# Attention and MoE on one core: the DMA transpose of a step issued behind the next step's write

## The chip, the cores and the metric

The kernel runs on one core of a Trainium2 chip. The metric is device time in microseconds (us) of one execution, lower is better. The core has five engines with a queue each, worked through in order: PE (TensorE, matrix products), ACT (ScalarE), DVE (VectorE), POOL (GpSimd) and SP (SyncE, which here only issues DMAs). An engine that waits for a semaphore holds everything that is queued behind the waiting instruction.

## The reference

Two layers, 8 batches, 8 heads, 512 local and 32 global positions, 64 elements per head. First windowed attention:

```python
s_g = scale * q_g @ k_all.T              # 32 global rows see all 544 columns
out_g = softmax(s_g) @ v_all
s_ll = where(|i - j| <= 32, scale * q_l @ k_l.T, -1e9)
s_l = concat([scale * q_l @ k_g.T, s_ll])  # 512 local rows: 32 global columns and the band
out_l = softmax(s_l) @ concat([v_g, v_l])
```

Then, over the 4608 rows of both (512 wide, heads side by side), `h = x @ w_in` (512x2048), `g = h * sigmoid(h)`, `g @ w_out` (2048x512), all in float32 results.

## The kernel before, in words

**Tiles and steps.** The 4608 rows are 36 tiles of 128 rows, worked in 12 blocks (`SIZES`: ten of 3 tiles, two of 2). A local tile is one batch `b` and one quarter `c` of the 512 positions; it takes 4 steps, one for each pair of heads (`pr`). So there are 128 steps `k`, and 16 of them make a batch.

**One step.** Its queries and keys are loaded (L343 or L345, `raw`), and from step 28 on split into a rounded part and a remainder: ACT casts `qk` (L365), DVE makes `klo` (L366) and the remainder of the queries (L367). PE makes the scores `s` (L381, or L383 and L384), DVE adds the mask (L388), ACT takes the exponential (L392), ACT and DVE scale (L399, L401, L403). The result `probs` has to be transposed for the second product.

**The transpose through DRAM.** Up to step 11 PE does it. From step 12 on (`KF`), POOL copies `probs` into two 16-bit planes (`halves`, L413, one buffer), SP writes these to DRAM (`away`, L418), and SP issues a DMA transpose that reads them back turned, into `pt` (`st_back`, L422; four `pt` buffers, one for each `pr`). A transpose waits for its own write to have landed. The one of `pr` 0 also waits until PE has read the `pt` of the tile before. When all four `pt` of a tile are there, PE makes the tile's 32 products `o` (L464), and ACT and DVE put them into the block's `x` (L471, L472, L478).

**The global rows.** For each batch the 32 global rows' probabilities `pg` are made during the batch before, in two halves `hh` (L250 to L297). From batch 3 on (`GD`) they too go through DRAM: `gaway` (L310) and a DMA transpose into `pgt` (L329). A rest of 32 columns is turned by PE (`gu`, L332) and copied by ACT into `pgu` (L335, two copies for each half).

**The MoE.** For each of 16 slices `f` of a block PE makes `h` (L625, 12 matmuls), ACT takes the tanh `t` (L632), DVE makes the product (L633), ACT rounds it to `gh` (L635), DVE takes the remainder `gl` (L636), and PE adds the three products to `out` (L652, 9 matmuls) one slice later. `x` and the weights are used as a rounded part and a remainder as well. During block 0 the weights are still being joined from loaded words and split (L221 to L234).

**What sets the order.** Attention steps of later blocks are laid between the MoE matmuls. Each part of step `k` has a due time, `at` of the step plus a number from the tables `DUE`, `DMAT`, `DMAT0` (and `TURN`, `TURND` for the two halves of a batch's global transpose); all parts are sorted by it, and this list is the program's order. On PE, and for the issues of DMAs on SP (`hold`), that order stands. On ACT, DVE and POOL a scheduler that plays the program through with estimated times puts it into an order of its own. The change edits the tables alone, and the orders of ACT, DVE and POOL follow from them.

Of the kernel before, what the change touches and what calls it, by code (L numbers as in the profile page):

```python
# [23 lines left out]
NPR = H // 2  # L24
# [37 lines left out]

DUE = dict(load=-1.2, split=-0.5, turn=1.6, out=2.2)
DMAT = dict(load=-1.65, halves=0.7, away=1.05, turn=1.3, back=1.65, out=2.7)
DMAT0 = dict(turn=1.75, back=1.95)
VLOADS = (None, -0.6, -1.0, 2.4)
BEFORE = 1.36
HEAD = dict(load=-0.9, split=0.2, scores=0.8, soft=1.0, halves=1.4, away=1.72, slot=0.3, later=1.6)
HEADS0, HEADS = (11, 1), (7, 2)
TURN1, TURN, TURND = (0.65, 1.5), (0.4, 1.5), (0.4, 0.45)  # L70
FULL = 0.98
END = 0.5

# [1 line left out]
def attention_moe_kernel(ctx: ExitStack, tc: tile.TileContext, qk0_in, qk_in, v_in, gqk, wts, out):  # L75
# [443 lines left out]
    def put(when, fn, *a):  # L519
        stream.append((when, fn, a))  # L520
# [3 lines left out]
    for k, (t, b, c, pr) in enumerate(steps):  # L524
        a = (k, b, c, pr)
        j = k % NST
        due = dict(DUE)
        if k >= KF:
            due.update(DMAT)
            due.update({} if pr else DMAT0)  # L530
        if WHOLE <= k < WHOLE + OWN:
            due["load"] = SOONER
        if k < AHEAD:
            due.update({part: FIRST[part][k] - k for part in ("load", "vload", "turn", "out")})
        elif pr == 0:
            due["vload"] = VLOADS[min(k // NPR, 3)]
        if k == AHEAD:
            for h in range(NPR):
                put(FIRST["gload"][h], g_load, 0, h)
                put(FIRST["gscores"][h], g_scores, 0, h)  # L540
            for hh in range(2):
                put(FIRST["gsoft"][hh], g_soft, 0, hh)
                put(FIRST["gturn"][hh], g_turn, 0, hh)
            put(FIRST["late"], g_late)
            at = FIRST["then"]
            for when in JOINS:
                put(at + when - NPR, join_weights)
            for f, when in enumerate(SPLITS):
                put(at + when - NPR, split_weights, f)
        if j == 0 and b:  # L550
            for hh in range(2):
                put(at + (TURN1 if b < 2 else TURN if b < GD else TURND)[hh], g_turn, b, hh)
        for f, half in FIRSTW.get(k, ()):
            put(at + 0.01, fetch_weights, f, half)
        ats.append(at)
        put(min(at + due["load"], ats[k - 3] + BEFORE) if k >= ND + 3 else at + due["load"], st_load, *a)
        put(at + due["split"], st_split, *a)
        put(at, st_scores, *a)
        if "vload" in due:
            put(at + due["vload"], st_vload, *a)  # L560
        if k >= KF:
            put(at + due["halves"], st_halves, *a)
            put(at + due["away"], st_away, *a)
        put(at + due["turn"], st_turn, *a)
        if k >= KF:
            put(at + due["back"], st_back, *a)
        if k < SINGLE or pr == NPR - 1:
            n = 1 if k < SINGLE else NPR
            put(at + due["out"], st_out, k - n + 1, n, b, c, t)
            marks[t] = at + due["out"]  # L570
        if j == NST - 1 and b % 4 == 3:
            put(marks[t] + 0.001, g_tile, t + 1)
            marks[t + 1] = marks[t] + 0.001
        if b + 1 < B:
            first, every = HEADS if b > 1 else HEADS0
            for h in [h for h in range(NPR) if first + h * every == j]:
                for part, fn in (("load", g_load), ("split", g_split), ("scores", g_scores)):
                    put(at + (SOONER if part == "load" and b + 1 < GF else HEAD[part]), fn, b + 1, h)
                if h % 2:
                    put(at + HEAD["later" if b == 0 else "soft"], g_soft, b + 1, h // 2)  # L580
                    if b + 1 >= GD:
                        put(at + HEAD["halves"], g_halves, b + 1, h // 2)
                        put(at + HEAD["away"], g_away, b + 1, h // 2)
                at += HEAD["slot"]
        at += 1.0
# [180 lines left out]
```

## Time and profile before

| what | value |
|---|---|
| median of 3 runs | 965.2 us (964.59 to 966.34) |
| the profiled execution | 964.87 us, span of its instructions 962.7 us |
| PE busy | 940.6 us, 98% of the span |
| PEld (weight loads, beside PE) | 840.9 us, 87% |
| DVE, ACT, POOL busy | 629.9, 574.2, 217.1 us |
| granted PE clock | full in all slices but the last |
| HBM traffic | 133 GB/s over the span |

Steps 0 to 11 and the start of the weights take the first 50 us, block 0 runs to about 140 us and the rest to the end is a steady mixture of MoE and attention. In rows of the timeline the columns are start (us from the span's start), duration, engine, line, operation, what it writes from what it reads, how many, and in brackets how long the engine had been idle and who ended that. In rows of waits they are the engine and line, what it waited for, microseconds in total, how often, and the longest. SPq is SP's queue.

### The profile page before, as it was taken

How to read it: one execution, taken by the hardware profiler on the slowest of the kernel's cores; microseconds unless marked ns; L12 is line 12 of the kernel's file. 1: busy time of each engine (PE TensorE's matmuls, PEld its weight loads, DVE VectorE, ACT ScalarE, POOL GpSimd, SP SyncE). 2: the span in 40 equal slices, each digit the busy share in tenths (PEclk: the TensorE clock that was granted, in tenths of full speed). 3: DMA queues.
4: the chain of work that ended last, by engine and by line, in shares of the span. 5: the costliest groups of instructions: out<-in, count | busy, mean ns of one | idle time of the engine just before them, and what ended most of it. 6: DMA issues, size and time to landing. Idle time of an engine off the chain costs nothing.

```text
span 962.7 us, 17396 instructions
## 1 busy us (share of the span) xinstructions
PE 940.6 (98%) x5734; PEld 840.9 (87%) x5734; DVE 629.9 (65%) x1893; ACT 574.2 (60%) x1475; POOL 217.1 (23%) x433
## 2 busy tenths in 40 slices
PE   8789999999999999999999999999999999999998
PEld 6578888999998999989999899998999899989897
DVE  5889977766876677655677677766677656453322
ACT  7888876656656566544665656665566555443322
POOL 2112322122332223122133222222223221120000
PEclk9999999999999999999999999999999999999999
DMA  8989966577668675743856776686775864532000
GB/s 301 350 226 262 266 170 187 158 171 213 172 157 211 168 192 147 193 116 86 223 158 167 201 172 188 159 206 170 170 216 148 201 147 130 144 93 66 1 22 23
DMA packets 201306, 162.57 MB, mean 169 GB/s; under 512 B 139392, under 2 KB 159360, under 8 KB 201216
## 3 DMA queue, kind: packets, MB, share of 16 engines
q1 hardware_dynamic: 196800, 153.52, 59.9%
q10 hardware_dynamic: 4416, 7.93, 2.3%
q8 instruction: 46, 0.75, 0.3%
q14 instruction: 44, 0.36, 0.1%
HBM read 86.44 MB, written 41.94 MB: 133 GB/s over the span
## 4 chain that ended last, share of the span: by engine, by line
PE 83%; DVE 4%; ACT 2%; issue 1%; DMA 0%; DVEq 0%; ACTq 0%
PE h L625 36%; PE out L652 35%; PE o L464 6%; PE s L383 2%; PE s L384 2%; DVE w_lo L234 1%; DVE w L224 1%; PE gs L275 1%; PE gs L276 1%; DVE probs L388 1%; DVE klo L366 0%; DMA raw<-in_qk_dram 0%; DVE raw_w L223 0%; ACT probs L392 0%; DVE t L633 0%
## 5 line engine op out<-in xcount | busy, mean ns | idle before, releaser
L413 POOL COPY halves<-probs 128x512 uint16<-128x512 uint16 x232 | 154.9, 694 | 436.2 <-ACT probs L399 234.6
L632 ACT ACTIVATE t<-h 128x384 f32<-128x384 f32 (+1 forms) x192 | 90.6, 472 | 172.5 <-PE h L625 156.9
L633 DVE SCALAR_TENSOR_TENSOR t<-t,h 128x384 f32<-128x384 f32 (+1 forms) x192 | 101.6, 529 | 105.9 <-ACT t L632 104.8
L652 PE MATMUL out<-w_hi,gh 128*128 128x512 f32 x544 | 164.2, 400 | 2.5 <-ACT gh L635 2.5
L625 PE MATMUL h<-xh,w_hi 128*128 128x384 f32 (+1 forms) x768 | 160.0, 330 | 1.9 <-ACT w_hi L233 1.9
L652 PE MATMUL out<-w_lo,gh 128*128 128x512 f32 x544 | 161.2, 394 | 0.0
L652 PE MATMUL out<-w_hi,gl 128*128 128x512 f32 x544 | 161.0, 394 | 0.0
L625 PE MATMUL h<-xl,w_hi 128*128 128x384 f32 (+1 forms) x768 | 158.2, 327 | 0.0
L625 PE MATMUL h<-xh,w_lo 128*128 128x384 f32 (+1 forms) x768 | 158.2, 327 | 0.0
L392 ACT ACTIVATE probs<-probs,st 128x224 f32<-128x224 f32 x244 | 115.8, 475 | 62.8 <-DVE st L388 62.1
L625 PEld LDWEIGHTS h<-xh,w_hi 128*128 128x128 f32 x768 | 132.9, 188 | 17.4 <-ACT w_hi L233 3.6
L636 DVE TENSOR_TENSOR gl<-t,gh 128x384 fp32r<-128x384 f32 (+1 forms) x192 | 110.3, 575 | 43.1 <-ACT gh L635 40.9
L388 DVE CUSTOM_DVE_ANT_0 probs<-s,mask 128x224 f32<-128x224 f32 x244 | 85.8, 387 | 80.2 <-PE s L384 70.8
L625 PEld LDWEIGHTS h<-xl,w_hi 128*128 128x128 f32 x768 | 132.8, 188 | 0.0
L625 PEld LDWEIGHTS h<-xh,w_lo 128*128 128x128 f32 x768 | 131.3, 188 | 0.5 <-DVE w_lo L234 0.3
L635 ACT CAST gh<-t 128x384 fp32r<-128x384 f32 (+1 forms) x192 | 94.5, 492 | 57.8 <-DVE t L633 57.6
L652 PEld LDWEIGHTS out<-w_hi,gl 128*128 128x128 f32 x544 | 100.3, 188 | 22.2 <-DVE gl L636 0.5
L652 PEld LDWEIGHTS out<-w_lo,gh 128*128 128x128 f32 x544 | 100.5, 188 | 21.7 <-issue 0.6
L652 PEld LDWEIGHTS out<-w_hi,gh 128*128 128x128 f32 x544 | 93.8, 189 | 13.3 <-ACT gh L635 4.7
L365 ACT CAST qk<-raw 128x704 fp32r<-128x704 f32 x100 | 77.5, 775 | 7.7 <-DMA raw<-in_qk_dram 5.2
L366 DVE TENSOR_TENSOR klo<-raw,qk 128x448 fp32r<-128x448 f32 x100 | 66.2, 662 | 18.2 <-ACT qk L365 16.7
L399 ACT ACTIVATE probs<-probs,st 128x224 f32<-128x224 f32 x118 | 56.7, 481 | 30.2 <-DVE st L395 28.7
(96 smaller groups left out, 1065.7 us busy)
## 6 DMA issues: line engine op xcount, KB each, us to landing
raw<-in_qk_dram SPq DMA_DIRECT2D x100, 352.0 KB, 3.2
away<-halves SPq DMA_DIRECT2D x116, 256.0 KB, 2.3
vraw<-in_v_dram SPq DMA_DIRECT2D x30, 512.0 KB, 5.1
raw_w<-in_wts_dram SPq DMA_DIRECT2D x29, 512.0 KB, 6.4
raw_g<-in_gqk_dram SPq DMA_DIRECT2D x32, 304.0 KB, 3.1
out_dram<-o ACTq DMA_DIRECT2D x29, 256.0 KB, 3.3
raw<-in_qk_dram SPq DMA_DIRECT2D x28, 240.0 KB, 4.6
gaway<-pg SPq DMA_DIRECT2D x10, 256.0 KB, 2.1
```

Of the source, the lines that this page charges most:

```text
L365: nc.scalar.copy(out=qk, in_=raw)
L366: nc.vector.tensor_tensor(out=klo[:, :KW], in0=raw[:, QW:], in1=qk[:, QW:].bitcast(F32), op=ALU.subtract)
L388: nc.vector.tensor_tensor_reduce(out=p[:, u, :W], in0=ss[u], in1=mask_of[c], scale=-SCALE, scalar=3.0e38, op0=ALU.add, op1=ALU.min, accum_ ...
L392: nc.scalar.activation(p[:, u, :W], p[:, u, :W], AF.Exp, bias=st[:, u : u + 1], scale=-1.0, accum_out=st[:, 2 + u : 3 + u])
L413: nc.gpsimd.tensor_copy(out=halves[:, :, u], in_=p[:, 2 * P * u : 2 * P * (u + 1)].bitcast(U16).rearrange("p (j h) -> p h j", h=2))
L464: nc.tensor.matmul(o[D * u : D * (u + 1), :m], vraw[:, a, u, :], pt[:, u, a, :m], start=(a == 0), stop=(a == 1))
L625: nc.tensor.matmul(h[:, :nt], wt[:, c * P : (c + 1) * P], x[:, c, :nt], start=(i == 0), stop=(i == 3 * NCC - 1))
L632: nc.scalar.activation(t[:, :nt], h[:, :nt], AF.Tanh, scale=0.5)
L633: nc.vector.scalar_tensor_tensor(out=t[:, :nt], in0=t[:, :nt], scalar=1.0, in1=h[:, :nt], op0=ALU.add, op1=ALU.mult)
L635: nc.scalar.copy(out=gh[:, :nt], in_=t[:, :nt])
L636: nc.vector.tensor_tensor(out=gl[:, :nt], in0=t[:, :nt], in1=gh[:, :nt].bitcast(F32), op=ALU.subtract)
L652: nc.tensor.matmul(outs[n][i], g[:, i * P : (i + 1) * P], w, start=(f == 0 and j == 0), stop=(f == NF - 1 and j == 2))
```

## The change

Three numbers of the tables. `back`, the issue of a step's DMA transpose, was due 1.65 steps after the step's own place (1.95 for `pr` 0), and is now due at 2.1, except for `pr` 3, the last of a tile, where it stays at 1.65. The next step's write `away` is due at 1 + 1.05 = 2.05. So the transposes of `pr` 0, 1 and 2 stand behind the next step's write. And the second half of the global transpose is due at 1.5 instead of 0.45, a step later than the first, from batch 3 on. It takes with it the DMA transpose into `pgt`, PE's `gu` and ACT's two `pgu` copies.

```diff
 DMAT = dict(load=-1.65, halves=0.7, away=1.05, turn=1.3, back=1.65, out=2.7)
-DMAT0 = dict(turn=1.75, back=1.95)
+DMAT0 = dict(turn=1.75)
+BACK = 2.1
...
-TURN1, TURN, TURND = (0.65, 1.5), (0.4, 1.5), (0.4, 0.45)
+TURN1, TURN, TURND = (0.65, 1.5), (0.4, 1.5), (0.4, 1.5)
...
         if k >= KF:
             due.update(DMAT)
             due.update({} if pr else DMAT0)
+            if pr < NPR - 1:
+                due["back"] = BACK
```

No instruction is added or taken away on PE; five `gu` transposes stand elsewhere. In the rows of the changed kernel the line numbers are 1 higher up to `st_back` and the like and 3 higher from the step loop on (L366 is L365 of before, L635 is L632, L423 is L422). The numbers behind an underscore at a name's end are the program's own, and the number in a name is the step, as in `raw29`, `qk50`, or block and slice, as in `t8_9`.

First place: SP's queue at steps 24 to 30, around 137 to 157 us. Before:

```order
L418 DMA away25_1786<-halves25_1766 128x1024
L241 DMA raw_g2_0_1788<-in_gqk_dram 128x608
L355 DMA vraw24_1817<-in_v_dram 128x4x256
L670 DMA out_dram<-o0_1846 128x512
L422 DMA_TRANSPOSE pt1_130<-away25_1786 128x4x256
L345 DMA raw28_1823<-in_qk_dram 128x704
L670 DMA out_dram<-o0_1846 128x512 x2
L418 DMA away26_1873<-halves26_1825 128x1024
L241 DMA raw_g2_1_1881<-in_gqk_dram 128x608
L422 DMA_TRANSPOSE pt2_131<-away26_1873 128x4x256
L345 DMA raw29_1934<-in_qk_dram 128x704
L418 DMA away27_1936<-halves27_1893 128x1024
```

And now:

```order
L423 DMA_TRANSPOSE pt0_129<-away24_1709 128x4x256
L242 DMA raw_g2_0_1788<-in_gqk_dram 128x608
L356 DMA vraw24_1817<-in_v_dram 128x4x256
L346 DMA raw28_1822<-in_qk_dram 128x704
L673 DMA out_dram<-o0_1845 128x512 x3
L419 DMA away26_1872<-halves26_1824 128x1024
L423 DMA_TRANSPOSE pt1_130<-away25_1785 128x4x256
L242 DMA raw_g2_1_1881<-in_gqk_dram 128x608
L346 DMA raw29_1933<-in_qk_dram 128x704
L419 DMA away27_1935<-halves27_1892 128x1024
L423 DMA_TRANSPOSE pt2_131<-away26_1872 128x4x256
L423 DMA_TRANSPOSE pt3_132<-away27_1935 128x4x256
```

The load `raw28` no longer stands behind a transpose and an output, and the load `raw29` no longer behind the transpose that waits for `away26` to land.

Second place: ACT's queue at steps 48 to 50, around 289 to 301 us, where batch 3's first tile begins (the second row and the third come once more where the first "..." stands). Before:

```order
L632 ACTIVATE t2_13_3598<-h2_13_3585 128x384
L392 ACTIVATE probs0_85,st48_3610<-probs0_85,st48_3610 128x224
L335 COPY pgu3_3629<-gu3_0_3631 32x64
...
L335 COPY pgu3_3629<-gu3_1_3636 32x64 x2
L635 CAST gh2_13_3599<-t2_13_3598 128x384
L399 ACTIVATE probs0_85<-probs0_85,st48_3610 128x224
L365 CAST qk49_3640<-raw49_3565 128x704
...
L399 ACTIVATE probs1_86<-probs1_86,st49_3680 128x224
L365 CAST qk50_3702<-raw50_3623 128x704
L632 ACTIVATE t2_15_3720<-h2_15_3707 128x384
```

And now:

```order
L635 ACTIVATE t2_13_3597<-h2_13_3584 128x384
L393 ACTIVATE probs0_85,st48_3609<-probs0_85,st48_3609 128x224
L336 COPY pgu3_3629<-gu3_0_3631 32x64
...
L638 CAST gh2_13_3598<-t2_13_3597 128x384
L400 ACTIVATE probs0_85<-probs0_85,st48_3609 128x224
L366 CAST qk49_3635<-raw49_3565 128x704
...
L400 ACTIVATE probs1_86<-probs1_86,st49_3675 128x224
L336 COPY pgu3_3629<-gu3_1_3698 32x64 x2
L635 ACTIVATE t2_15_3720<-h2_15_3707 128x384
L366 CAST qk50_3702<-raw50_3623 128x704
L638 CAST gh2_15_3721<-t2_15_3720 128x384
```

Two of the four `pgu` copies have moved a step on, and there the cast `qk50` now stands behind the tanh `t2_15`. At steps 80 to 82 (batch 5) the rows have moved in the same way.

Third place: ACT's queue at steps 112 and 113, around 749 to 753 us, the first tile of batch 7. Before:

```order
L635 CAST gh8_8_8947<-t8_8_8946 128x384
L335 COPY pgu7_8980<-gu7_0_8982 32x64 x2
L399 ACTIVATE probs0_85<-probs0_85,st112_8958 128x224
L335 COPY pgu7_8980<-gu7_1_8990 32x64 x2
L365 CAST qk113_8994<-raw113_8916 128x704
L632 ACTIVATE t8_9_9012<-h8_9_8999 128x384
```

And now:

```order
L638 CAST gh8_8_8946<-t8_8_8945 128x384
L336 COPY pgu7_8980<-gu7_0_8982 32x64 x2
L400 ACTIVATE probs0_85<-probs0_85,st112_8957 128x224
L635 ACTIVATE t8_9_9007<-h8_9_8994 128x384
L366 CAST qk113_8989<-raw113_8916 128x704
L638 CAST gh8_9_9008<-t8_9_9007 128x384
```

The two copies are gone from here, and the cast `qk113` stands behind the tanh `t8_9`, which waits for the matmuls of `h8_9`. On DVE the product of `t8_9` (L633) has likewise moved ahead of `klo113` (L366).

## The prediction

> **What bounds the kernel now.** I read the page first, then PE's waits, then 25 us windows to see where PE idles, then the timeline of those places on all engines.
>
> ```profile
> PE 940.6 (98%) x5734; PEld 840.9 (87%) x5734; DVE 629.9 (65%) x1893; ACT 574.2 (60%) x1475; POOL 217.1 (23%) x433
> PE s L383 <- DVE qk L367: 3.0, 3, 1.3
> PE h L625 <- ACT w_hi L233: 1.9, 3, 1.1
> PE gs L275 <- DVE acc L478: 1.1, 1, 1.1
> SPq L418 <- POOL halves L413: 166.0, 84, 8.4
> SPq L422 <- DMA away<-halves: 102.9, 68, 5.3
> SPq L422 <- PE o L464: 91.7, 23, 10.0
> 100.00:125.00 25.00, 24.71 (x144) 21.83 (x144) 23.35 (x67) 21.09 (x54) 7.43 (x12) 1.00 0.90 259
> 150.00:175.00 25.00, 23.76 (x146) 21.07 (x145) 19.25 (x58) 16.25 (x42) 5.83 (x13) 1.00 0.70 179
> 275.00:300.00 25.00, 23.75 (x129) 21.32 (x128) 18.01 (x53) 15.60 (x42) 5.27 (x8) 1.00 0.78 191
> 750.00:775.00 25.00, 24.46 (x151) 21.84 (x150) 15.70 (x47) 14.22 (x37) 6.94 (x12) 1.00 0.83 197
> ```
>
> PE is busy 940.6 of 962.7 us, at the full clock (the 1.00 in the windows). No row has PE waiting for a DMA transpose or for `pt`. SP's queue stands hundreds of microseconds, 102.9 of them for the write that a transpose reads, but that is idle time of a queue that PE is not waiting for. So what the change saves on SP is worth only what it does to PE's few gaps: 1.24 us near 165, 1.25 near 295 and as much near 535, 0.54 near 754, and the `w_hi` waits of block 0. Most of the other idle time lies before step 12, which the change doesn't touch. At most 5 us can be won; new gaps have no such limit.
>
> **The change part by part.** The sum is made against the profiled execution's own 964.87 us, 0.3 below the median 965.2.
>
> *The transposes themselves.* A transpose holds SP while it is issued and lands some microseconds later.
>
> ```profile
> L422 SPq DMA_TRANSPOSE pt<-away x116: 1226/1228/2913, 53.9 to 879.4; - x116
> DMA to landing us min/median/max: 2.9/3.6/8.8
> 506.08 1.23 SPq L422 DMA_TRANSPOSE pt<-away  x1
> 509.20 2.18 PE L464 MATMUL o<-pt,vraw 128*64 128x160 f32 x32
> ACT qk L365 <- DMA raw<-in_qk_dram: 5.2, 5, 1.7
> ```
>
> Those of `pr` 0 to 2 go about a step later; they are used when the whole tile is there, one to three steps on, so they have room. The critical one is that of `pr` 3, which does not move but now has `pr` 2's 1.23 us of issue between its write and itself. In most tiles this lies in the wait for its own write, which it has anyway. The tightest late tile I found is the one above: issued 506.08, plus the median 3.6 gives 509.7, and its products are the last 8 of the 32, begun at 509.20 + 24/32 x 2.1 = 510.8. It has 1.1 us to spare. Cost: nothing, covered by these waits; if a tile's cover is gone, 1.23 us. The loads that are queued behind a moved transpose go up to 1.23 us later. Only 5 of 100 casts waited for their load, so I count nothing, except where a load goes earlier (next).
>
> *The loads of steps 28 and 29*, the first place of the order.
>
> ```profile
> 141.67 1.29 SPq L422 DMA_TRANSPOSE pt<-away  x1
> 143.06 0.52 SPq L345 DMA_DIRECT2D raw<-in_qk_dram  x1
> 148.97 1.23 SPq L422 DMA_TRANSPOSE pt<-away  x1
> 150.37 0.46 SPq L345 DMA_DIRECT2D raw<-in_qk_dram  x1
> 148.46 0.42 DVE L367 TENSOR_TENSOR qk<-raw,qk 64x256 fp32r<-64x256 f32 x1
> 155.33 0.99 DVE L366 TENSOR_TENSOR klo<-raw,qk 128x448 fp32r<-128x448 f32 x1 [2.16 <-ACT qk L365]
> 164.98 0.21 DVE L478 TENSOR_TENSOR acc<-o,acc 128x64 f32<-128x64 f32 x1
> 165.34 0.36 PE L275 MATMUL gs<-qk_g 128*128 128x272 f32 x1 [1.14 <-DVE acc L478]
> ```
>
> `raw29` went at 150.37, behind a transpose that waited for its write. Its buffer was free at 148.88, when L367 of step 28 ended, and that may come 0.4 earlier since `raw28` goes at about 142.6. So `raw29` can go at about 148.5, some 1.9 us sooner. DVE had idled 2.16 us for that load and then worked without a break up to the `acc` that PE waits for. 1.9 us less backlog there covers both gaps, 1.14 and 0.10. I take -1.2; the bounds are -1.24 and 0, if something else that DVE waits for there comes no sooner.
>
> *The `pgu` copies*, the second place, where batch 3 begins; steps 80 to 82 in batch 5 are its like.
>
> ```profile
> L335 ACT COPY pgu<-gu x32: 185/200/203, 17.3 to 751.3; 32x64 f32<-32x64 f32 x32
> 292.91 0.76 ACT L365 CAST qk<-raw 128x704 fp32r<-128x704 f32 x1
> 295.35 0.34 PE L383 MATMUL s<-qk 128*128 128x224 f32 x1 [1.25 <-DVE qk L367]
> 300.25 0.49 ACT L632 ACTIVATE t<-h 128x384 f32<-128x384 f32 x1 [0.95 <-PE h L625]
> 302.46 0.37 PE L383 MATMUL s<-qk 128*128 128x224 f32 x1
> L366 DVE TENSOR_TENSOR klo<-raw,qk x100: 606/625/1061, 147.8 to 852.2; 128x448 fp32r<-128x448 f32 x100
> L367 DVE TENSOR_TENSOR qk<-raw,qk x100: 422/422/739, 148.5 to 852.8; 64x256 fp32r<-64x256 f32 x100
> ```
>
> ACT had no pause ahead of the cast at 292.91, so two copies fewer bring it, and the scores of step 49, 0.41 us forward: a gap of about 1.0 instead of 1.25 (PE is itself 0.12 sooner without the second `gu`). A step later the bill comes. `qk50` now stands behind `t2_15`, which waits for PE. That tanh began at 300.25, now 300.25 - 0.41 + 0.12 = 299.96; the cast can start 0.39 behind it, at 300.35, takes 0.77, then L366 0.63, L367 0.42 and 0.17 between them: scores possible at 302.34. PE is ready for them at 302.46 - 0.41 + 0.12 = 302.17. So 0.17 of the gain is lost again in a new wait, and 0.12 is kept. Twice: -0.2, between -0.6 (nothing lost) and +0.6 (L366 at its longest, 1.061).
>
> *Step 113*, the third place, the same move with no room at all.
>
> ```profile
> 751.48 0.78 ACT L365 CAST qk<-raw 128x704 fp32r<-128x704 f32 x1
> 752.62 0.49 ACT L632 ACTIVATE t<-h 128x384 f32<-128x384 f32 x1 [0.36 <-PE h L625]
> 753.81 0.34 PE L383 MATMUL s<-qk 128*128 128x224 f32 x1 [0.54 <-DVE qk L367]
> ```
>
> The cast began at 751.48 and its scores were already 0.54 late. Now it follows `t8_9`, which cannot begin before PE has finished `h8_9`: 752.62 - 0.12 = 752.50. So the cast at 752.89, plus 0.77, 0.63, 0.42 and 0.18 between them up to PE's start: 754.9 instead of 753.81, +1.1. Behind these scores stands all of PE's queue, so the loss stays. Bounds: +0.9, if nothing is lost between these four, and +1.9, with L366 at 1.061 and L367 at 0.739.
>
> *Other casts that moved*: `qk53` and `qk85` now follow `gh` and, on DVE, `gl`.
>
> ```profile
> 318.13 0.77 ACT L365 CAST qk<-raw 128x704 fp32r<-128x704 f32 x1
> 318.81 0.51 ACT L635 CAST gh<-t 128x384 fp32r<-128x384 f32 x1
> 320.60 0.26 PE L383 MATMUL s<-qk 128*128 128x224 f32 x1
> ```
>
> The cast starts 0.51 later, at 318.64, and 0.77 + 0.63 + 0.42 + 0.17 later it is 320.63, against 320.60 without a wait: nothing, up to +0.4 each.
>
> *Block 0.* From about 100 to 130 us ACT's and DVE's orders are shuffled: weight work ahead, `gh` behind. DVE has 23.35 us of work in 25 there, and that amount is unchanged.
>
> ```profile
> 130.29 0.96 PE L625 MATMUL h<-xh,w_hi 128*128 128x384 f32 x4 [0.55 <-ACT w_hi L233]
> ```
>
> Weights sooner can save the gap at 130 and a smaller one, 0.8 together; `gh` later can cost as much. I take 0, from -0.8 to +1.0.
>
> The sum: 0 - 1.2 - 0.2 + 1.1 + 0 + 0 = -0.3, so 964.6 by the profiled execution's count and 964.9 on the median's.
>
> **The rivals.** *Faster, 0.19: block 0's gain comes whole and little is lost again.* 965.2 - 0.8 (block 0) - 1.2 - 0.6 + 0.9 = 963.5, and 962.6 if step 113 also loses nothing. For it: weight casts are what PE waits for in block 0, and they now stand earlier. Against it: step 113's cast can't pass `t8_9` in ACT's queue.
>
> *Slower, 0.15: the moved casts' DVE work meets POOL's copies.* The rows of L366 and L367 show two speeds, 0.625 and up to 1.061, 0.422 and up to 0.739. Moving a cast a microsecond or two puts its L366 under another `halves` copy of POOL. If it is slow at each of the five places, it costs 1.9 at 113, 0.6 at 49 to 50 and 81 to 82 together, and 0.4 each at 53 and 85: 3.3, and 965.2 + 3.3 - 0.3 = 968.2, with 0.9 of the 1.2 lost in the same way near 165. It decides from three slow ones on. Against it: the median is the fast one. [...]
>
> *Slower, 0.09: the last transpose of a tile comes late.* In three tight tiles like that of 509 us, 1.23 of issue and, as an estimate, as much again in landing behind `pr` 2's traffic, less the 1.1 to spare: 1.4 each, 4.1 in all, 969.0. For it: landings reach 8.8 us. Against it: in the row above, the transpose at 506.08 stood behind a load, not behind its write, so `pr` 2's is hidden there.
>
> *That nothing changes on PE*, since only SP's idle time moves, is 965.2 and lies inside the forecast.
>
> **How the numbers follow.** A measurement of this kernel tells about 0.2%, 1.9 us, from no change. The forecast, 964.9 with its own range 963.3 to 967.1, has 0.57. Faster is the first rival with its 0.19, slower the two others, 0.15 + 0.09. The range for 8 in 10 reaches into both sides: 962.6 (the first rival with nothing lost at step 113) to 968.2 (the second rival).
>
> **What would show it.** At step 113 (near 754 us) a PE wait for L367 of 1.4 to 1.9 us instead of 0.54; near 295 and 535 about 1.0 instead of 1.25, and new waits under 0.8 at steps 50 and 82; no `gs` wait for `acc` near 165; SP's waits for `away` far below 102.9. It is wrong if PE waits for a transpose or for `pt` at any L464, if block 0 ends more than a microsecond sooner or later than 132, or if the gap at 165 stays while `raw29` goes sooner.

## The result and the profile after

The changed kernel takes 972.8 us (median of 6, 971.22 to 974.92) against 966.05 (6 runs, 964.59 to 967.92) of the kernel before beside it: ratio 1.0071, 95% interval 1.0058 to 1.0085. It is slower by 6.8 us, where 964.9 was forecast. Its profiled execution took 971.22 us, with a span of 969.4 instead of 962.7.

What PE waited for in the changed kernel (total, times, longest; only the rows that bear on the change, the others lie before 60 us). Its line numbers are higher by 1, and by 3 from the step loop on:

```profile
PE s L384 <- DVE qk L368: 5.3, 5, 1.7
PE h L628 <- ACT w_hi L234: 3.7, 4, 2.0
PE out L655 <- DVE gl L639: 0.6, 2, 0.3
PE o L465 <- DMA pt<-away: 0.5, 1, 0.5
PE gs L276 <- DVE acc L479: 0.2, 1, 0.2
```

What SP waited for, the row of POOL's copies and the row of the transposes' own writes:

```profile
SPq L419 <- POOL halves L414: 300.0, 83, 10.1
SPq L423 <- DMA away<-halves: 12.8, 15, 4.0
```

The same four windows as before (PE, PEld, DVE, ACT and POOL busy, then granted clock, DMA share, GB/s):

```profile
100.00:125.00 25.00, 23.88 (x138) 20.68 (x138) 22.74 (x66) 19.08 (x48) 5.47 (x10) 1.00 0.89 250
150.00:175.00 25.00, 24.80 (x156) 22.65 (x156) 20.29 (x59) 15.97 (x40) 6.29 (x13) 1.00 0.79 216
275.00:300.00 25.00, 23.85 (x128) 21.20 (x127) 18.99 (x54) 14.41 (x39) 7.12 (x10) 1.00 0.67 166
750.00:775.00 25.00, 23.26 (x144) 20.59 (x143) 15.09 (x49) 13.96 (x40) 5.90 (x12) 1.00 0.83 201
```

On SP the wait for a transpose's own write fell from 102.9 to 12.8 us, but the wait for POOL's copies rose from 166.0 to 300.0: SP mostly waits for something else now. PE is busy 0.8 us less in the first window, 1.0 more in the second, 0.1 more in the third and 1.2 less in the last. Its waits grew: casts 3.0 to 5.3, `w_hi` 1.9 to 3.7, and two kinds are new, `gl` and `pt`. Laid matmul against matmul, the two profiled executions come apart at these places:

| place (before), us | what PE waits for, before and after | time lost |
|---|---|---|
| 108 | last `pt` of the tile of steps 16 to 19, 0 and 0.53 | +0.7 |
| 119 to 134 | `w_hi` casts, and matmuls at half the clock (granted 0.50) | +3.3 |
| 163 to 165 | `gs` for `acc` (and 0.10 for `qk_g`), 1.24 and 0.20 | -1.2 |
| 286, 526 | `out` for `gl`, 0 and about 0.3 | +1.1 |
| 295, 535 | scores of steps 49, 81, 1.25 each and 0.82, 1.02 | -0.7 |
| 302, 542 | scores of steps 50, 82, 0 and 0.88 each | +1.9 |
| 320, 560 | scores of steps 53, 85, 0 and 0.14 | +0.6 |
| 754 | scores of step 113, 0.54 and 1.74 | +1.2 |

That is 6.9; many small steps take back 0.2. More than half, 4.0 (0.7 and 3.3), is block 0, which the forecast had at zero. Here is the end of its chain of waits after (start, us, what), up to the longest wait of PE for `w_hi`:

```profile
124.28 0.29 DVE probs L389
...
124.58 0.30 DVE probs L389
...
124.89 0.34 DVE w L225
125.23 0.46 DVE t L636
125.69 0.07 DVE st L396
...
125.89 0.18 DVE st L396
...
126.14 0.48 ACT probs L400
126.62 0.26 ACT probs L402
...
126.89 0.61 ACT w_hi L234
...
127.55 1.68 PE h L628 x5
```

The cast `w_hi14` is held in program order behind the softmax scaling of step 23 (L400, L402). That needs a reciprocal (L396, which ends in the row at 125.69; the one at 125.89 is step 24's), and DVE now does it behind the scores of step 24, a weight join (L225) and the product for `t0_13` (L636). The scaling also stands behind the cast `gh0_13`, which needs that product and ended at 126.23, so these rows do not tell which of the two held it longer. On ACT the exponentials of step 23 come later too, at 122.35 instead of 119.49, behind two casts of `w_hi` and three weight joins. In the kernel before, that reciprocal stood ahead of the joins of `w14`:

```profile
121.16 0.17 DVE L395 RECIPROCAL st<-st 128x2 f32<-128x2 f32 x1
...
122.35 0.69 DVE L224 SCALAR_TENSOR_TENSOR w<-w,raw_w 128x512 uint32<-128x512 uint32 x1
```

The windows right behind this wait (columns as above):

```profile
127.00:128.00 1.00, 0.45 (x2) 0.45 (x3) 0.47 (x1) 1.00 (x3) 0.90 (x2) 0.96 0.02 8
128.00:129.00 1.00, 1.00 (x4) 1.00 (x4) 1.00 (x3) 1.00 (x4) 0.00 (x0) 0.50 0.21 80
...
130.00:131.00 1.00, 1.00 (x5) 1.00 (x4) 0.90 (x4) 0.00 (x0) 0.00 (x0) 0.50 2.00 82
131.00:132.00 1.00, 1.00 (x7) 1.00 (x5) 0.14 (x1) 0.50 (x2) 0.05 (x1) 0.83 0.36 72
```

For some 3.4 us PE ran at half clock, granted 0.50: its matmuls came every 0.32 us instead of 0.18. From the end of the wait on, the two executions come 1.4 us further apart, so about 1.4 of the 3.3 us is this.

### The profile page after: what moved, and what is told of

Same layout as the page of the kernel before. It is cut to its first block, busy times and chain, and to the rows that moved or that the text cites. A ratio compares the mean times of both kernels' runs of the same rounds, so it can differ in the third digit from the quotient of the medians.

```text
span 969.4 us, 17383 instructions
## 1 busy us (share of the span) xinstructions
PE 942.9 (97%) x5734; PEld 842.3 (87%) x5734; DVE 630.6 (65%) x1893; ACT 573.1 (59%) x1475; POOL 216.5 (22%) x433
## 4 chain that ended last, share of the span: by engine, by line
PE 79%; DVE 6%; ACT 4%; issue 1%; DMA 0%; DVEq 0%; ACTq 0%
PE h L628 34%; PE out L655 34%; PE o L465 5%; PE s L384 2%; PE s L385 2%; ACT probs L393 1%; DVE qk L368 1%; DVE w L225 1%; DVE probs L389 1%; ACT qk L366 1%; DVE klo L367 1%; DVE gl L639 1%; PE gs L276 1%; PE gs L277 1%; ACT probs L400 0%
## 5 line engine op out<-in xcount | busy, mean ns | idle before, releaser
L635 ACT ACTIVATE t<-h 128x384 f32<-128x384 f32 (+1 forms) x192 | 90.6, 472 | 179.9 <-PE h L628 172.3
L636 DVE SCALAR_TENSOR_TENSOR t<-t,h 128x384 f32<-128x384 f32 (+1 forms) x192 | 101.6, 529 | 114.0 <-ACT t L635 113.3
L639 DVE TENSOR_TENSOR gl<-t,gh 128x384 fp32r<-128x384 f32 (+1 forms) x192 | 107.4, 560 | 41.8 <-ACT gh L638 39.7
L366 ACT CAST qk<-raw 128x704 fp32r<-128x704 f32 x100 | 77.5, 775 | 4.0 <-DVE pg L279 1.5
L400 ACT ACTIVATE probs<-probs,st 128x224 f32<-128x224 f32 x118 | 56.9, 482 | 34.3 <-DVE st L396 30.9
L367 DVE TENSOR_TENSOR klo<-raw,qk 128x448 fp32r<-128x448 f32 x100 | 67.4, 674 | 13.2 <-ACT qk L366 11.1
```

Source lines behind the costliest of these rows:

```text
L366: nc.scalar.copy(out=qk, in_=raw)
L367: nc.vector.tensor_tensor(out=klo[:, :KW], in0=raw[:, QW:], in1=qk[:, QW:].bitcast(F32), op=ALU.subtract)
L400: nc.scalar.activation(p[:, 0, :W], p[:, 0, :W], AF.Copy, scale=st[:, 6:7])
L635: nc.scalar.activation(t[:, :nt], h[:, :nt], AF.Tanh, scale=0.5)
L636: nc.vector.scalar_tensor_tensor(out=t[:, :nt], in0=t[:, :nt], scalar=1.0, in1=h[:, :nt], op0=ALU.add, op1=ALU.mult)
L639: nc.vector.tensor_tensor(out=gl[:, :nt], in0=t[:, :nt], in1=gh[:, :nt].bitcast(F32), op=ALU.subtract)
```

## The experiments

Theory A of the runs: moved transposes cost nothing themselves; the planner orders ACT's and DVE's queues anew from the edited tables, and at some places that order makes PE wait. Rivals put the loss on late transfers, on the global turn, or on a lack of room on DVE. All kernels are the one before with an edit, with its line numbers. Ratios are to the kernel before, run beside them.

### The parts alone

```diff
-TURN1, TURN, TURND = (0.65, 1.5), (0.4, 1.5), (0.4, 0.45)
+TURN1, TURN, TURND = (0.65, 1.5), (0.4, 1.5), (0.4, 1.5)
```

> Only the second part of the change: the global turn of the second pair of heads pairs a step later, the transposes of the steps as in the kernel before. Theory A (the loss comes from the order of the ACT and DVE queues, part by part, and mostly from the first part): the two score waits of steps 49 and 81 (295 and 535 us) shrink by about 0.4 us each, because two pgu copies no longer stand ahead of the casts there, and steps 50 and 82 pay that back at most; step 113 keeps a wait of 0.5 us or less; block 0 and the gap at 165 us stay as before. 965.0 to 966.5 us, ratio 0.999 to 1.0005. Rival B (the global turn itself is what costs it, its transpose and copies arriving late): 968 to 970 us with waits of pt or gu on the PE after 290 and 530 us.

Measured: 965.12 us, ratio 0.9987 (0.9979 to 0.9995). The second part alone makes it a little faster. The waits at 295 and 535 are 0.94 instead of 1.25, and steps 50 and 82 pay nothing.

The next two move the transposes of part of the steps; the first has this line, the second `k >= ND` in it:

```diff
-            due.update({} if pr else DMAT0)
+            due.update({} if pr else DMAT0); due.update({'back': 2.1} if pr < NPR - 1 and k < ND else {})
```

> Only the transposes of steps 12 to 27 moved, the rest as before. Theory A: block 0 loses its whole 4.0 us here (0.7 at 108 us where o waits for the last transpose of a tile, about 3.3 at 119 to 132 us where h waits for w_hi), and the gap at 165 us goes (-1.2): +2.8, 968.9 us, ratio 1.003; nothing differs behind 170 us. Rival C (block 0's loss comes from the changes of later steps, through the shared planner, or was noise of one execution): 964.8 us.

Measured: 968.15 us, ratio 1.0022 (1.0007 to 1.0037). Both losses of block 0 are there, the first larger than in the whole change, the second smaller: a wait of 1.45 instead of 2.02, with no half-clock stretch behind it, the granted clock being 1.00 from 100 to 134 us (PE's waits behind 100 us):

```profile
PE o L464 <- DMA pt<-away: 1.9, 1, 1.9
PE h L625 <- ACT w_hi L233: 1.7, 2, 1.5
PE gs L275 <- DVE acc L478: 0.6, 1, 0.6
```

Matmul against matmul, block 0 loses 2.7 us here.

> Only the transposes of steps 28 and later moved, the rest as before. Theory A: block 0 and the gap at 165 us as before; the casts of steps 50, 82 and 113 stand behind a tanh on ACT, which costs about 1.2 us at 753 us and 0.5 to 1.0 us at each of 302 and 542 us, and the second layer waits 0.3 to 0.6 us for gl at 286 and 526 us: +2.5 to +4, 968.5 to 970 us, ratio 1.0026 to 1.004. Rival B (the transposes' own lateness): waits of o for pt on the PE behind 170 us. Rival D (the later half is harmless alone, only the two parts together cost it): 965.5 to 966.5 us.

Measured: 969.13 us, ratio 1.0027 (1.0015 to 1.0039). The step-113 wait is 1.74 and the `gl` waits 0.18 and 0.26, but at steps 50 and 82 there is only 0.11 each. The parts add up to less than the whole: behind 170 us their profiled executions gain 1.1 and lose 2.4, the whole change loses 4.1. Of the missing 2.8, 0.77 at each of these two places and 0.3 each at steps 53 and 85, 2.1 in all, come only with both. The reason stands in the rows of step 50, first after, then with the late steps alone:

```profile
302.92 0.49 ACT L635 ACTIVATE t<-h 128x384 f32<-128x384 f32 x1 [1.29 <-PE h L628]
303.30 0.77 ACT L366 CAST qk<-raw 128x704 fp32r<-128x704 f32 x1
304.10 1.56 POOL L414 COPY halves<-probs 128x512 uint16<-128x512 uint16 x2
304.11 1.08 DVE L367 TENSOR_TENSOR klo<-raw,qk 128x448 fp32r<-128x448 f32 x1
305.20 0.73 DVE L368 TENSOR_TENSOR qk<-raw,qk 64x256 fp32r<-64x256 f32 x1
306.08 0.34 PE L384 MATMUL s<-qk 128*128 128x224 f32 x1 [0.88 <-DVE qk L368]
```

```profile
302.94 0.63 DVE L366 TENSOR_TENSOR klo<-raw,qk 128x448 fp32r<-128x448 f32 x1
303.58 0.42 DVE L367 TENSOR_TENSOR qk<-raw,qk 64x256 fp32r<-64x256 f32 x1
```

With both parts the cast ends just as POOL begins its `halves` copies, and both DVE instructions run slow: 1.08 + 0.73 instead of 0.63 + 0.42, 0.76 more. That is the whole difference of the two waits. At step 53 of the changed kernel the second of the two is slow in the same way, 0.74 instead of 0.42, and that is the 0.3 lost there (step 85 has the same 0.74):

```profile
323.37 1.41 POOL L414 COPY halves<-probs 128x512 uint16<-128x512 uint16 x2 [4.76 <-ACT probs L400]
323.57 0.74 DVE L368 TENSOR_TENSOR qk<-raw,qk 64x256 fp32r<-64x256 f32 x1
```

Of the 42 slow ones in the whole changed kernel (16 of L367 at 0.77 to 1.08, 26 of L368 at 0.73 to 0.74) 38 overlap a `halves` copy and all of them some copy of POOL's; of the 158 fast ones 20 overlap a `halves` copy, and 38 some copy of POOL's. No run moved POOL's copies alone, so that they are the cause rests on these rows and this count.

### The casts

To the whole change an issue order is added on ACT, and no wait (`queued` tells the planner that an instruction is issued behind a named one):

```diff
-        nc.scalar.copy(out=qk, in_=raw)
+        lead["qk", k] = nc.scalar.copy(out=qk, in_=raw)
...
-        nc.scalar.activation(t[:, :nt], h[:, :nt], AF.Tanh, scale=0.5)
+        queued(nc.scalar.activation(t[:, :nt], h[:, :nt], AF.Tanh, scale=0.5), ('qk', QUEUED.get((n, f))))
+QUEUED = {(2, 15): 50, (5, 15): 82, (8, 9): 113}
```

> The whole change, with an issue order added on ACT alone: the tanh of slices 2_15, 5_15 and 8_9 stands behind the casts of steps 50, 82 and 113, as in the kernel before. No wait is added, and PE, POOL and SP keep the changed kernel's order. Theory A: the wait at 753 us falls from 1.74 to 0.5 us (-1.2) and those at 302 and 542 us from 0.88 each to 0.5 or less (-0.4 to -0.9 each): 970.0 to 970.9 us against 972.8, ratio to before 1.004 to 1.005. Rival B (loads and transposes land late there, the order on ACT is only what shows): the three waits stay, 972.8 us.

Measured: 972.68 us, ratio 1.0055 (1.0034 to 1.0075). The waits at steps 50 and 82 are gone, that at 113 is 0.08 instead of 1.74: 3.4 us less at these places. The median gained only 1.5 us against the ratio 1.0071, and the two intervals overlap; the profiled execution had three half-clock stretches where the changed kernel's had one: 0.50 at 44 to 46 and at 58 to 60 us, and a mean of 0.79 over 132 to 140. Matmul against matmul it loses 0.9 us behind 170 us, where the whole change loses 4.1. So the places settle it, the total doesn't.

### Block 0

One transpose moved, with `k == 16` in the line above:

> One transpose moved, that of step 16, behind the write of step 17; the transposes of steps 17 to 19, the last of that tile among them, stand where they stood before. On ACT and DVE this alone gives the order of the changed kernel around w_hi14 (the softmax of step 24 and the cast gh0_13 ahead of it). Theory A (the order on ACT and DVE is what costs it at 124 us): h still waits 1.2 to 2.0 us for w_hi near 124 us, though o no longer waits for pt at 108 us; 967 to 968.5 us, ratio 1.001 to 1.002. Rival E (the late last transpose at 108 us shifts everything behind it, and the wait at 124 us follows from that): no wait over 0.6 us at 124 us, 966.3 us.

Measured: 968.42 us, ratio 1.0029 (1.0013 to 1.0046). There is no wait for `pt`, and `h` waits 1.71 us at 119 and 2.03 at 124. So the `w_hi` waits don't follow from the late transpose.

With `20 <= k < ND`:

> Only the transposes of steps 20 to 27 moved. Theory A (steps 12 to 19 make the loss of block 0, steps 24 to 26 the gain at 165 us): no wait for pt at 108 us, waits for w_hi as before (at most 1.1 us, at 130 us), the wait of gs near 165 us 0.8 to 1.2 us shorter: 965.1 to 965.5 us, ratio 0.9988 to 0.9992. Rival F (any moved transpose in the weights' phase costs): 967 us or more.

Measured: 965.74 us, ratio 0.9998 (0.9988 to 1.0009). Block 0 is as before, so its loss belongs to steps 12 to 19. The gap at 165 is 1.27, and this half of the expectation fell. But the run did not bring the load forward: `raw29` was issued at 150.05 instead of 150.37 and landed at 155.49 instead of 154.44. So it does not test what an earlier load gives.

With `k < 16`, which moves steps 12 to 14 (that of 15 is the last of its tile) and nothing on any other engine:

> Three transposes moved, those of steps 12 to 14; this changes the order on SP alone, and no instruction of PE, ACT, DVE or POOL changes its place. Theory A (a moved transpose costs nothing by itself; its cost comes through the queue orders that the planner derives from it, and through a last transpose that lands behind it): no wait of the PE differs by more than 0.3 us behind 60 us, 965.5 to 966.4 us, ratio 0.9995 to 1.0005. Rival F (each moved transpose costs through the loads behind it): about 0.2 to 0.5 us each, 966.6 to 967.5 us.

Measured: 966.9 us, ratio 1.0005 (0.9993 to 1.0017), no difference. The median lies in rival F's range, but the kernel before took 966.36 beside it, and the ratio is theory A's. No wait behind 60 us changed by more than 0.35.

With `k < ND and k != 18`:

> The transposes of steps 12 to 27 moved but for that of step 18, which stays ahead of the write of step 19. Theory A (the last transpose of that tile lands late because that of step 18 was moved right in front of the transfers it has to share the queues with): the wait of o for pt at 108 us, 1.94 us with step 18 moved, falls to 0.3 or less, and the waits for w_hi stay at 1.4 us or more. Rival I (the weights' loads, which now stand ahead of it in a denser row, set it): the wait stays above 0.5 us.

Measured: 968.47 us, ratio 1.0022 (1.0011 to 1.0034). The wait for `pt` is gone, the `w_hi` waits are 1.78 and 2.02. SP's rows show it, first with step 18's transpose moved, then with it in its old place; the last row of each is the transpose of step 19:

```profile
99.17 1.30 SPq L422 DMA_TRANSPOSE pt<-away  x1
100.51 1.04 SPq L205 DMA_DIRECT2D raw_w<-in_wts_dram  x2
101.66 0.38 SPq L343 DMA_DIRECT2D raw<-in_qk_dram  x1
102.13 2.60 SPq L422 DMA_TRANSPOSE pt<-away  x1
```

```profile
97.43 1.23 SPq L422 DMA_TRANSPOSE pt<-away  x1
99.21 0.35 SPq L418 DMA_DIRECT2D away<-halves  x1
99.61 0.92 SPq L205 DMA_DIRECT2D raw_w<-in_wts_dram  x2
100.63 0.38 SPq L343 DMA_DIRECT2D raw<-in_qk_dram  x1
103.53 1.23 SPq L422 DMA_TRANSPOSE pt<-away  x1
```

The two transposes and three loads leave SP within 3 us, and the last one holds SP for 2.60 us instead of 1.23 and lands at 110.25; in the second kernel it is issued 1.4 us later and lands at 107.27.

Then the order on DVE was mended in steps. First the reciprocal of step 23 alone, ahead of the scores of step 24 and of `t0_13`:

```diff
+        lead['st', k] = nc.vector.reciprocal(out=st[:, 6:8], in_=st[:, 4:6])
...
+            queued(nc.vector.tensor_tensor_reduce(...), ('st', 23) if k == 24 else None)
...
+        queued(nc.vector.scalar_tensor_tensor(out=t[:, :nt], ...), ('st', 23) if (n, f) == (0, 13) else None)
```

> The transposes of steps 12 to 27 moved, as in the run of the early steps, with an issue order added on DVE: the reciprocal of step 23 ahead of the scores of step 24 and of the product for t0_13. No wait is added, SP keeps its order. Theory A: the cast of w_hi14, which stands behind the softmax of step 23 on ACT, comes about 1.5 us earlier, and the wait near 124 us falls from 1.45 us to 0.6 or less, while o still waits for pt at 108 us: 0.9 to 2 us less than without the order, 966.2 to 967.3 us. Rival E (the wait follows from the late transpose): the wait near 124 us stays at 1.4 us, 968.2 us.

Measured: 969.06 us, ratio 1.0038 (1.0025 to 1.0051). The wait at 124 fell to 0.55 as expected, and a wait of 2.00 us came up one slice later, at `w_hi15`, behind the same order at steps 24 and 25. The time was only moved on. With the reciprocals of steps 22 to 25 all ordered so:

> As the run that put the reciprocal of step 23 first, but now the reciprocals of steps 22 to 25 all stand on DVE ahead of the next step's scores and of the product of slices 0_12 to 0_14. Theory A (the wait is the order alone; with one step mended the same order came back a step later): no wait for w_hi over 0.6 us behind 110 us, o still waits 1 to 2 us for pt at 108 us; 966.3 to 967.8 us, ratio 1.0 to 1.0015. Theory G (DVE has no room left there, whatever the order): waits for w_hi of 1.5 us or more together remain; 968.5 us or more.

The conditions are then `('st', k - 1) if 23 <= k <= 26` and `('st', f + 10) if n == 0 and 12 <= f <= 14`. Measured: 968.25 us, ratio 1.0018 (1.0005 to 1.0032). The `w_hi` waits behind 110 us are 1.04, 0.69 and 0.70, as theory G has it, and `o` waits 0.36 for a copy of POOL's and no longer for a transpose. But the reciprocals still stood behind the weights' joins there, as the chain shows:

```profile
122.26 0.52 ACT w_hi L233
...
123.64 0.68 DVE w_lo L234
...
124.76 0.69 DVE w L224
...
126.74 0.07 DVE w L224
...
127.04 0.17 DVE st L395
...
127.30 0.48 ACT probs L399
127.78 0.37 ACT probs L401
128.15 0.52 ACT w_hi L233
```

It is a loop: a cast of `w_hi`, its `w_lo`, the joins of the next weight, the reciprocal, the softmax, the next cast, 5.9 us a turn. From `h0_13` to `h0_14` the kernel before takes 4.9 us, and from there to `h0_15` 5.9, of which 0.55 is a wait. So engines with idle time can still set the pace: of the 22 us from 108 to 130 DVE is busy for 19.75 and ACT for 18.01 in the changed kernel. Two runs cut the loop. One leaves out the second half of the joins of two weights, on top of the transpose of step 16:

```diff
-        hold(nc.vector.scalar_tensor_tensor(out=wi, in0=wi, scalar=3, in1=low, ...))
+        hold(nc.vector.scalar_tensor_tensor(out=wi, in0=wi, scalar=3, in1=low, ...)) if whole else None
```

> The transpose of step 16 moved, as in that run, and the second half of joining the words of w13 and w14 left out on DVE (six instructions, about 2.6 us together); the two weights are then not the reference's. Theory G (DVE has no room left between 110 and 130 us, so each order that lets it wait costs the PE): the waits of h for w_hi at 119 and 124 us (1.71 and 2.03 us) and the next one fall below 0.6 us together, and the stretch to 134 us ends 2 to 4 us earlier: 964.5 to 966.5 us. Rival H (the weights' transfers, which land up to 1 us later, set it): the waits stay above 1 us each.

Measured: 965.88 us, ratio 0.9997 (0.9985 to 1.0008), by the two ratios 3.1 us below the run with step 16 alone. Of the waits for `w_hi`, 0.28 is left at 119 us, nothing at 124, and 0.70 at 130, where the kernel before has 0.55: together 1.0, more than the 0.6 expected, but not the over 1 us each of rival H. Leaving work out also changed the order, so this run shows that a shorter loop fits, not why. The other leaves all work in, with steps 12 to 27 moved, and writes the joins behind the slice's attention work:

```diff
-                while w_next[0] < 2 * min(NF, f + LOOK):
+                while f not in (11, 12, 13) and w_next[0] < 2 * min(NF, f + LOOK):
...
             fill(SIZES[n])
+            while n == 0 and f in (11, 12, 13) and w_next[0] < 2 * min(NF, f + LOOK):
+                join_weights()
```

> The transposes of steps 12 to 27 moved as in the run of the early steps; the joining of weights 13 to 15 is written behind the attention work of its slice, so that on ACT and DVE the softmax of steps 22 and 23 stands ahead of it again, as in the kernel before. PE and, up to the outputs' place, SP keep the order of the early-steps run. Theory A (the order alone closes the loop from the cast of w_hi over w_lo, the joins, the reciprocal and the softmax to the next cast): the waits for w_hi behind 110 us fall to 0.8 us together, o still waits 1 to 2 us for pt at 108 us: 966.0 to 967.5 us, ratio 0.9998 to 1.0012. Theory G (DVE has no room there in any order): waits for w_hi of 1.5 us or more together, 968.2 us, ratio 1.002.

Measured: 967.4 us, ratio 1.0020 (1.0009 to 1.0031). PE's waits behind 100 us:

```profile
PE out L652 <- ACT gh L635: 1.3, 1, 1.3
PE o L464 <- DMA pt<-away: 1.1, 1, 1.1
PE h L625 <- ACT w_hi L233: 1.1, 2, 0.8
```

Behind 110 us a single wait for `w_hi` of 0.80 is left, which theory A gave, with all the work and all transposes moved. So the wait came from the order, not from the amount of work. The ratio is above the forecast, at theory G's 1.002. Matmul against matmul, block 0 loses 1.9 us, 1.3 of it at the late `pt`, which was expected, and 0.6 at `w_hi`. The new wait of `out` for `gh`, 1.28 at 158 us, is given back right behind it: the gap at 165 is 0 instead of 1.24.

### The account, and a faster kernel

The whole change without the transposes of steps 12 to 19 (`k >= 20`), and with the casts ordered as above:

> The whole change but for the transposes of steps 12 to 19, which stay where they stood before, with the issue order on ACT that keeps the casts of steps 50, 82 and 113 ahead of the tanh. Theory A (these two things make the whole loss): waits of w_hi and pt in block 0 as before, score waits of about 0.9 us at 295 and 535 us and under 0.3 us at the three steps, waits for gl of 0.3 us at 286 and 526 us left: 965.3 to 966.3 us, ratio 0.9990 to 1.0003. If something else costs it too: 967.5 us or more.

Measured: 967.19 us, ratio 1.0008 (0.9995 to 1.0021), no longer told apart from the kernel before. Of 0.7% about 0.6 is explained by these two places. The ratio is 0.5 us above the top of the expected range. There are new waits, 0.39 for a `pt` copy of POOL's at 108 and 0.66 at 149, and the gap at 165 is gone. Matmul against matmul, the kernel loses 0.1 us from 107 us to the end; the 1.9 us by which its profiled execution is late lie before 60 us, where it has a half-clock stretch (0.50 from 55 to 58).

The second part, with the transpose of step 25 alone (`k == 25`):

> The second part of the change as a whole, and of the first part the transpose of step 25 alone, behind the write of step 26 and the load of step 28. Theory A (what gains and what loses lie at separate places): three score waits 0.3 us shorter each (295, 535, 754 us) and the wait of gs near 165 us about 1.0 us shorter, block 0 as before: 964.0 to 964.6 us, ratio 0.9977 to 0.9984, faster than both. Rival: the gain at 165 us is eaten by another wait right behind it, 965.1 us, ratio 0.9987.

Measured: 963.9 us, ratio 0.9978 (0.9968 to 0.9988), faster than both kernels. The gap at 165 is 1.05, and against PE `raw29` lands only 0.2 us sooner, so step 25 gives next to nothing, and this is about the second part alone; the two intervals overlap.

The second part with the casts of steps 49 and 81 ahead of a softmax scaling:

```diff
-            nc.scalar.activation(p[:, 0, :W], p[:, 0, :W], AF.Copy, scale=st[:, 6:7])
+            queued(nc.scalar.activation(p[:, 0, :W], p[:, 0, :W], AF.Copy, scale=st[:, 6:7]), ('qk', k + 1 if k in (48, 80) else None))
...
+            due.update({'split': -1.02} if k in (49, 81) else {})
```

> The second part of the change alone, with the casts of steps 49 and 81 issued on ACT ahead of the normalization of steps 48 and 80 (six rows of ACT change place, no other engine's). Theory A (the queue order on ACT sets these score waits): they fall from 0.94 to 0.55 us each, 0.8 us less than the second part alone: ratio 0.9979 (0.997 to 0.9987), 963.9 us. Rival: DVE's klo takes its slow form beside POOL or stands behind gl, and the waits stay at 0.9 us: ratio 0.9987.

Measured: 964.21 us, ratio 0.9979 (0.9969 to 0.9990), as expected; the waits are 0.44 and 0.45. It, too, beats both kernels.

## Why the prediction was wrong, point by point

- **Block 0: "I take 0, from -0.8 to +1.0"**: the step that failed, +3.3 (4.0 with the late transpose of the next point). The working looked at the amount of work on DVE, which did not change, and priced only the waits in view. It did not follow the new order round the loop: the cast of `w_hi` is held behind a softmax that in its turn had been put behind the joins. Its own test, block 0 ending over a microsecond later, shows it wrong. Of the 3.3, about 1.4 are half-clock matmuls behind a 2.0 us wait, which no term had.
- **The transposes, "nothing"**: right for each by itself (steps 12 to 14: ratio 1.0005), wrong for one tile. "The tightest late tile I found" was not the tightest: in the kernel before, the last transpose of steps 16 to 19 landed at 108.01 and its products began at 108.15. It cost 0.7 us, inside the 1.23 named for a tile whose cover is gone. The third rival had the mechanism at 0.09; it holds at one tile, for 0.5 us in the changed kernel and up to 1.9 in another run.
- **The `pgu` copies, -0.2**: +1.2, outside the bounds of -0.6 and +0.6. Steps 49 and 81 came as worked out, gaps of 0.82 and 1.02 for about 1.0. The bill at steps 50 and 82 was 0.88 each, not 0.17. This is what the second rival named, slow L366 and L367 beside POOL: 0.45 and 0.31 us longer at step 50, while POOL's two `halves` copies took 1.56. With steps 53 and 85, where L367 alone was slow (0.74 for 0.42), it came at four of its five places, for 2.1 us in all.
- **Step 113, +1.1**: right, +1.2, with both DVE instructions fast. Ordering the cast first took it away.
- **Steps 53 and 85, "nothing, up to +0.4 each"**: 0.3 each, inside the bound, all of it the slow L367.
- **`gl` at 286 and 526**: in no term, +1.1. They come with the late steps alone; what in the queues delays `gl` there was not tried.
- **The loads of steps 28 and 29, -1.2**: the number came; whether it came for the reason given stays open. Counted against PE, `raw29` was issued 2.5 us sooner and landed 2.0 sooner, and DVE's pause of 2.16 ahead of its L366 shrank to 0.09, as worked out. But PE was 3.8 us late by then, and in the run with less work, where these loads keep their old order, the gap is 0 as well. Every kernel in which it shrank by more than 0.2 had lost 1 us or more between 107 and 160 us, and no run brought the load clearly forward without such a loss. So it may in part be block 0's loss given back. How much for which loss is open too: others that lost as much keep 0.56 to 0.95.

Right were that SP's waits are worth nothing by themselves, and that new gaps have no limit where the gains have one, though the gaps listed there add up to 6.2 us and not 5.

## What to carry to other kernels

When a table edit lets a planner reorder queues, follow each moved row round its loop: what is held behind it, what that feeds, and when the loop comes back; equal work on an engine says nothing on the loop's length. List the spare time of every tile or slice before calling a move covered, for the one left out will be the one that decides. A wait that shrinks may only be an earlier loss given back: test it with the early loss taken away, and see in that run that what was to come sooner does come sooner.

## What had not been expected of the hardware

After a pause PE was sometimes granted half the clock (0.50) for about 3.4 us, which, as an estimate from these two numbers, costs 1.7 us. In the 17 profiled executions there were 22 pauses of 2.0 us or more on PE behind 20 us, 17 of them of 2.5 us near 55 us that every kernel has, and 5 of 2.0 us in block 0; 5 of the 17 and 3 of the 5 came with such a stretch behind them (in one run it began within the pause). The drop at each kernel's very end is left aside. None of the 8 pauses from 1.45 to 1.94 us had one. Two more stretches stood behind a row of pauses of up to about 1 us near 41 us. The times spread with the clock: the kernel with only the early steps moved ran between 965.68 and 972.56 us, its executions at a mean clock of 1.000 near 966.2 and those at 0.995 or less near 972.4.
